# Turning K on VectorE in 32x32 blocks instead of on TensorE, in a decode step with a cached attention window

## The chip, the cores and the metric

One core of one Trainium2 chip. The metric is the device time of one execution in microseconds (us), the median of several executions. The kernel before takes 384.67 us (384.57 to 384.93 in 4 executions). The kernel before ran again in every round of experiments and took 384.67 to 384.78 us each time, so medians of different rounds can be set side by side.

## The reference, cut to what matters

```python
B, Sq, D = 4, 1, 576;  Hq, Hkv, Sk, Dh = 32, 16, 16384, 128     # bf16
W = min(4096, max(256, Sk // 4))                                # 4096 keys are looked at
q = (layernorm(x) @ wq)                                         # 32 heads of 128
k = k_cache[:, :, Sk - W:, :] ; v = v_cache[:, :, Sk - W:, :]   # each serves two q heads
p = softmax(q @ k.T * Dh ** -0.5) ;  o = p @ v
h = x + o @ wo
out = h + ((relu(n @ W_gate) * (n @ W_up)) @ W_down)            # n = layernorm(h)
```

Nearly all bytes are the window of K and V: 4 batches of 16 heads of 4096 keys of 128 values, 134 MB of the 160 MB that are read.

## The kernel before

K and V come in tiles of 4 MB (four heads of one batch), through a ring of four slots in SBUF. Partition `4*p + a` of a tile holds 128 keys of head `a`, one after the other (a load row of 32 KB).

```python
src = cache[b, 4*qd:4*qd+4, SK-WIN:SK, :].rearrange("a (p t) d -> p a (t d)", p=32)
place((kind, g), off, TILE, ("TR", 4*g+3) if kind == "K" else ("PV", 4*g+3),   # who frees the slot
      lambda e: e.dma_start(out=arena[:, off:off+TILE], in_=src), key=f"slot{s}")
```

QK needs K with the head dimension on the partitions. TensorE turns K in 128x128 pieces, and a permutation in place of the identity also sorts the keys by head. VectorE and ScalarE copy the pieces from PSUM to SBUF by turns:

```python
pe(("TRJ", i, j), lambda e: e.transpose(out=bankb[TRB[j]][:, u*128:(u+1)*128], in_=kn[:, t, :],
                                        identity=perm.rearrange("p a k -> p (a k)")), deps)      # L425
if j % 2 == 0: dve(("EV", i, j), lambda e: e.tensor_copy(out=dst, in_=src), deps)                # L439
else:          act(("EV", i, j), lambda e: e.copy(out=dst, in_=src), deps)                       # L441
# QK: 32 columns of q, four matmuls abreast in four column groups
bank[4+w][32*j:32*j+32, :], lhsT=qTm[:, b, 4*qd+a, :], rhs=k[:, j, :, a, :]                      # L457
# P: exp writes every score four times, TensorE turns it, VectorE masks it while copying
dve(("PM", b, r), lambda e: e.tensor_tensor(out=dst, in0=src, in1=msk, op=ALU.mult), ...)        # L487
```

[... cut: constants, projections of q, softmax weights, output selection, the gated layer ...]

Of the kernel before, what the change touches and what calls it, by code (L numbers as in the profile page):

```python
# [6 lines left out]
ALU = mybir.AluOpType  # L7
# [4 lines left out]
B = 4  # L12
# [9 lines left out]
NUNIT = 4 * NTILE  # L22
# [5 lines left out]
KTW = 8192  # L28
# [86 lines left out]
def bass_sequential_preLN__sliding_block_cached__glu_gated_reglu__decode_kernel(  # L115
# [12 lines left out]
    with ExitStack() as es:  # L128
# [12 lines left out]
        arena = sb("arena", [128, 2 * KTW + NSLOT * TILE], BF16)  # L141
# [6 lines left out]
        c_m4 = sb("c_m4", [128, 4, 32], FP32)  # L148
        c_qm = sb("c_qm", [128, 4, 32], FP32)
        c_e8 = sb("c_e8", [128, 8, 16], FP32)  # L150
        c_s4 = sb("c_s4", [128, 4, 4], FP32)
        perm = sb("perm", [128, 4, 32], BF16)
        m4 = sb("m4", [128, 4], FP32)
        par = sb("par", [128, 2], FP32)
        am8 = sb("am8", [128, 8], FP32)
# [16 lines left out]
        qTm = sb("qTm", [128, B, KVH, 32], BF16)  # L172
        stat = sb("stat", [128, B, 8], FP32)
        gm4 = sb("gm4", [1, 128], FP32)
        fq = sb("fq", [128, 4], FP32)
# [19 lines left out]

        kT = [arena[:, i * KTW:(i + 1) * KTW] for i in range(2)]
        slot0 = 2 * KTW

# [3 lines left out]
        TRB = (0, 1, 2, 3)  # L202
        s_ps = psb[:, 4:6, :].rearrange("p a b -> p (a b)")
        o_ps = bank[6]
        m_ps = bank[7]
        mb_ps = bankb[7]
# [25 lines left out]
        def add_kv(kind, g):  # L232
            b, qd = divmod(g, 4)
            s = ring_slot()
            off = slot0 + s * TILE
            cache = A_k_cache if kind == "K" else A_v_cache
            src = cache[b, 4 * qd:4 * qd + 4, SK - WIN:SK, :].rearrange("a (p t) d -> p a (t d)", p=32)
            place((kind, g), off, TILE, ("TR", 4 * g + 3) if kind == "K" else ("PV", 4 * g + 3),
                  lambda e: e.dma_start(out=arena[:, off:off + TILE], in_=src), key=f"slot{s}")
# [19 lines left out]
        for blk in range(2 * KTW // 64):  # L259
            owner[blk] = "QKEND"  # L260
# [24 lines left out]
        def kv(kind, i):  # L285
            off = land[(kind, i // 4)]
            return arena[:, off:off + TILE].rearrange("p (t d) -> p t d", d=DH)

# [5 lines left out]
        pool("c_perm0", lambda e: e.memset(perm[:, :, :], 0.0))  # L294
        pool("c_perm", lambda e: e.affine_select(out=perm[:, :, :], in_=perm[:, :, :], pattern=[[-1, 4], [-4, 32]],
                                                 compare_op=ALU.not_equal, fill=1.0, base=0, channel_multiplier=1), ["c_perm0"])
# [6 lines left out]
                                                compare_op=ALU.not_equal, fill=1.0, base=0, channel_multiplier=1), ["c_m40"])  # L303
        pool("c_ones", lambda e: e.memset(ones_f[:, :], 1.0))
# [20 lines left out]
        for j in range(4):  # L325
            pool(f"c_same{j + 1}", lambda e, j=j: e.affine_select(out=sameh[:, :, :], in_=sameh[:, :, :], pattern=[[0, 4], [-1, 32]],
                                                                compare_op=ALU.not_equal, fill=0.25, base=-32 * j,
                                                                channel_multiplier=1), [f"c_same{j}"])

        pool("c_toq0", lambda e: e.memset(toq[:, :, :, :], 0.0))  # L330
        for q in range(4):
# [10 lines left out]
        dve("c_am8", lambda e: e.tensor_copy(out=am8[:, :].rearrange("p (a h) -> p a h", h=2),  # L342
                                             in_=bass.AP(tensor=m4, offset=0, ap=[[4, 128], [1, 4], [0, 2]])), ["c_m4"])
        dve("c_qTm", lambda e: e.memset(qTm[:, :, :, :], 0.0))
# [23 lines left out]
        def pe_q():  # L368
# [4 lines left out]
            for c in range(DC):  # L373
                pe("TP1", lambda e, c=c: e.transpose(out=tpv[:, 32 + c * 4:32 + (c + 1) * 4],
                                                     in_=chunk(x_bf, xd_bf[:, :, :].rearrange("b r a -> b (r a)"), c),
                                                     identity=ident_b[0:B, 0:B]))
            for c in range(DC):
# [7 lines left out]
            for bk in range(2):  # L385
                for s in range(4):
                    blk = bk * 4 + s
                    pe(("QT", blk), lambda e, blk=blk: e.transpose(out=mb_ps[:, blk * 128:(blk + 1) * 128],
                                                                   in_=p_sb[:, blk * 128:(blk + 1) * 128], identity=ident_b[:, :]),
                       [f"qev{bk}"] if s == 0 else [])  # L390

        def dve_q():
# [5 lines left out]
            dve("xT", lambda e: e.tensor_copy(out=xT[:, :, :], in_=tpv[:, 32:52].rearrange("p (c b) -> p c b", b=B)))  # L398
            dve("qev0", lambda e: e.tensor_copy(out=p_sb[:, 0:512], in_=bank[4]), ["QMM"])
            for s in range(8):  # L400
                hh4, bk = s % 4, s // 4
                off = 34 * (bk * 8 + hh4 // 2) + hh4 % 2
                dst = bass.AP(tensor=qTm, offset=off, ap=[[B * KVH * 32, 128], [68, 4], [KVH * 32, B]])
                dve("qTm", lambda e, dst=dst, s=s: e.tensor_copy(  # L404
                    out=dst, in_=mb_ps[:, s * 128:(s + 1) * 128].rearrange("p (g b) -> p g b", b=32)[:, :, 0:4]),
                    [("QT", 7), "c_qTm"])
# [5 lines left out]
        def pe_tr(i):  # L412
            kn = kv("K", i)
            for j in range(4):
                for u in range(8):
                    t = j * 32 + i % 4 * 8 + u
                    deps = []
                    if u == 0:
                        deps = [("L", "K", i // 4)] if j == 0 else []
                        if i == 0:  # L420
                            deps.append("c_perm")
                        else:
                            deps.append(("EV", i - 1, j))
                    last = j == 3 and u == 7
                    o = pe(("TRJ", i, j), lambda e, j=j, u=u, t=t: e.transpose(  # L425
                        out=bankb[TRB[j]][:, u * 128:(u + 1) * 128], in_=kn[:, t, :],
                        identity=perm[:, :, :].rearrange("p a k -> p (a k)")), deps)
                    if last:
                        P.names[("TR", i)] = o

        def evac(i, j):
            lo = j * 2048 + i % 2 * 1024
            dst = kT[i // 2 % 2][:, lo:lo + 1024]
            src = bankb[TRB[j]][:, 0:1024]
            deps = [("TRJ", i, j)]
            if i >= 4:
                deps.append(("QK", i // 2 - 2))
            if j % 2 == 0:
                dve(("EV", i, j), lambda e: e.tensor_copy(out=dst, in_=src), deps)  # L439
            else:  # L440
                act(("EV", i, j), lambda e: e.copy(out=dst, in_=src), deps)  # L441

        def pe_qk(dd):
            g, w = divmod(dd, 2)
            b, qd = divmod(g, 4)
            k = kT[dd % 2].rearrange("p (j t a k) -> p j t a k", j=4, t=16, a=4)
            for a in range(4):
                for j in range(4):
                    deps = []
                    if a == 0:  # L450
                        deps.append(("EV", 2 * dd + 1, j))
                        if qd == 0 and j == 0:
                            if b == 0:
                                deps += ["qTm", "qev0", "qev1"]
                            else:
                                deps += [("EXP", b - 1, w), ("MAX", b - 1)]
                    o = pe(("QK", dd), lambda e, a=a, j=j: e.matmul(  # L457
                        bank[4 + w][32 * j:32 * j + 32, :], lhsT=qTm[:, b, 4 * qd + a, :], rhs=k[:, j, :, a, :],
                        start=(qd == 0 and a == 0), stop=(qd == 3 and a == 3), skip_group_check=True), deps)
            P.names["QKEND"] = o  # L460

        def softmax(b, w):
            if w == 0:
                dve(("MAX", b), lambda e: e.tensor_reduce(out=stat[:, b, 0:1], in_=s_ps, axis=AX.X, op=ALU.max, negate=True),  # L464
                    [("QK", 8 * b + 7)])
                dve(("NB", b), lambda e: e.tensor_scalar(out=stat[:, b, 1:2], in0=stat[:, b, 0:1], scalar1=SCALE, scalar2=None,  # L466
                                                         op0=ALU.mult), [("MAX", b)])
            act(("EXP", b, w), lambda e: e.activation(  # L468
                out=p_sb[:, 2048 * w:2048 * w + 2048].rearrange("p (k a) -> p k a", a=4),
                in_=bass.AP(tensor=psb, offset=(4 + w) * 512, ap=[[4096, 128], [1, 512], [0, 4]]), func=ACT.Exp,  # L470
                bias=stat[:, b, 1:2], scale=SCALE, accum_out=stat[:, b, 2 + 3 * w:3 + 3 * w]),
                [("NB", b), ("PT", b - 1, 3) if b else ("QT", 7)])

        def put_pT(b, r):
            for tl in range(8):
                deps = []
                if tl == 0:
                    deps = [("EXP", b, r // 2)]
# [246 lines left out]
```

## Time and profile before

| | before |
|---|---|
| time, median | 384.67 us |
| load queue busy, share of 16 engines' span | 97.4% |
| mean rate of the loads | 418 GB/s |
| PE, VectorE (DVE), ScalarE (ACT) busy | 65%, 42%, 38% |

These are lines of the profile's page of the kernel before. In the second part of the page each digit is the busy share of one of 40 slices of the span, in tenths. The groups at the end have columns: line, engine, operation, output from input, shapes, count, then busy time (us) and mean ns of one, then the idle time of the engine just before them and what ended most of it.

```profile
PE 248.7 (65%) x3781; PEld 185.9 (49%) x3781; DVE 159.0 (42%) x277; ACT 146.4 (38%) x162; POOL 8.7 (2%) x36
...
DVE  3342565665342434774432426752516454002220
...
DMA  8999999999999999999999999999999999999992
GB/s 329 439 433 432 410 421 437 434 433 433 425 423 433 427 433 435 427 420 433 437 430 435 424 428 427 427 428 439 437 432 415 421 436 451 416 431 426 416 411 113
...
q1 hardware_dynamic: 6352, 159.59, 97.4%
...
DMA 69%; PE 27%; DVE 2%; SPq 1%; ACT 1%; issue 0%
...
L425 PE MATMUL psb<-sb_perm,sb_arena 128*128 128x128 bf16 x2048 | 140.3, 235 | 74.0 <-DMA sb_arena<-in_A_k_cache_dram 73.8
L441 ACT COPY sb_arena<-psb 128x1024 bf16<-128x1024 bf16 x128 | 123.0, 1021 | 141.1 <-PE psb L425 141.1
...
L439 DVE COPY sb_arena<-psb 128x1024 bf16<-128x1024 bf16 x128 | 87.0, 689 | 112.1 <-PE psb L425 111.6
...
L512 DVE TENSOR_TENSOR sb_o_tmp<-psb,sb_qm 128x512 f32<-128x512 f32 x16 | 11.1, 692 | 41.2 <-PE psb L505 41.2
L487 DVE TENSOR_TENSOR sb_pp<-psb,sb_am 128x1024 bf16<-128x1024 bf16 x16 | 19.6, 1223 | 16.2 <-PE psb L480 16.2
...
L516 DVE TENSOR_REDUCE sb_o_sel<-sb_o_tmp 128x128 f32<-128x512 f32 x16 | 16.4, 1024 | 0.5
```

The loads never stop: the DMA row is 9 from the second slice to the last but one. PE waits for K's loads (74 us before L425); the issue of loads waits for free slots too (144.7 us on L425), but it runs so far ahead (a K tile lands 28.3 us after its issue in the median, a V tile 33.6) that the loads themselves never run out. L512 and L516 handle the same 512 elements per partition. L512 reads them in order and takes 0.69 us; L516 reads its SBUF input at a stride of 512 bytes and takes 1.02 us.

One line of the groups by shape: 32 bf16 values written 64 bytes apart took 0.29 us.

```profile
L560 DVE CAST sb_oT<-psb 128x32 bf16<-128x32 f32 x4 | 1.2, 292 | 0.8 <-PE psb L556 0.8
```

### The profile page before, as it was taken

Reading aid. Unit: us, or ns where it says so; the run is one execution under the profiler, and the core shown is the slowest. Engines: PE = TensorE matmul, PEld = TensorE weight load, DVE = VectorE, ACT = ScalarE, POOL = GpSimd, SP = SyncE. Lnnn points to the kernel's source line nnn. Section 1 sums busy time; section 2 is a strip of 40 time slices with the busy share of each in tenths; the row PEclk is TensorE's granted clock in tenths of the full one; section 3 lists DMA queues with packets and bytes.
Section 4 is the critical chain, followed back from the end, with each engine's and each line's share of the span. In section 5 each row is a group of like instructions: output and inputs, shape, how many; then the busy total and the mean of one; then the engine's idle time right before and its main releaser. Section 6 shows DMA issues by size and latency. Waiting matters only on the chain.

```text
span 382.6 us, 8170 instructions
## 1 busy us (share of the span) xinstructions
PE 248.7 (65%) x3781; PEld 185.9 (49%) x3781; DVE 159.0 (42%) x277; ACT 146.4 (38%) x162; POOL 8.7 (2%) x36
## 2 busy tenths in 40 slices
PE   0664999779492938893947667966759366026753
PEld 0643788557371726672726455745546222003532
DVE  3342565665342434774432426752516454002220
ACT  3341688836161524762433428542525401000010
POOL 7100000000000000000000000000000000000000
PEclk9997999999888796999796969996969657555597
DMA  8999999999999999999999999999999999999992
GB/s 329 439 433 432 410 421 437 434 433 433 425 423 433 427 433 435 427 420 433 437 430 435 424 428 427 427 428 439 437 432 415 421 436 451 416 431 426 416 411 113
DMA packets 6408, 160.09 MB, mean 418 GB/s; under 512 B 740, under 2 KB 744, under 8 KB 1384
## 3 DMA queue, kind: packets, MB, share of 16 engines
q1 hardware_dynamic: 6352, 159.59, 97.4%
q8 instruction: 29, 0.48, 0.5%
q14 instruction: 3, 0.02, 0.0%
q10 hardware_dynamic: 24, 0.01, 0.0%
HBM read 159.58 MB, written 0.00 MB: 417 GB/s over the span
## 4 chain that ended last, share of the span: by engine, by line
DMA 69%; PE 27%; DVE 2%; SPq 1%; ACT 1%; issue 0%
DMA sb_arena<-in_A_k_cache_dram 53%; PE psb L425 18%; DMA sb_arena<-in_B_W_down_dram 8%; DMA sb_arena<-in_A_v_cache_dram 8%; PE psb L457 5%; PE psb L505 2%; PE psb L480 1%; DVE sb_pp L487 1%; ACT sb_pp L468 1%; SPq L280 0%; DVE sb_stat L464 0%; DVE sb_o_sel L516 0%; PE psb L539 0%; PE psb L530 0%; DVE sb_o_tmp L512 0%
## 5 line engine op out<-in xcount | busy, mean ns | idle before, releaser
L425 PE MATMUL psb<-sb_perm,sb_arena 128*128 128x128 bf16 x2048 | 140.3, 235 | 74.0 <-DMA sb_arena<-in_A_k_cache_dram 73.8
L441 ACT COPY sb_arena<-psb 128x1024 bf16<-128x1024 bf16 x128 | 123.0, 1021 | 141.1 <-PE psb L425 141.1
L425 PEld LDWEIGHTS psb<-sb_perm,sb_arena 128*128 128x128 bf16 x2048 | 131.5, 106 | 89.3 <-DMA sb_arena<-in_A_k_cache_dram 79.8
L439 DVE COPY sb_arena<-psb 128x1024 bf16<-128x1024 bf16 x128 | 87.0, 689 | 112.1 <-PE psb L425 111.6
L505 PE MATMUL psb<-sb_arena,sb_pp 128*32 128x512 bf16 x512 | 35.9, 425 | 19.9 <-DMA sb_arena<-in_A_v_cache_dram 19.9
L457 PE MATMUL psb<-sb_arena,sb_qTm 128*32 128x512 bf16 x512 | 38.0, 423 | 0.9 <-DVE sb_qTm L404 0.9
L505 PEld LDWEIGHTS psb<-sb_arena,sb_pp 128*32 128x32 bf16 x512 | 12.9, 104 | 36.3 <-DMA sb_arena<-in_A_v_cache_dram 20.9
L512 DVE TENSOR_TENSOR sb_o_tmp<-psb,sb_qm 128x512 f32<-128x512 f32 x16 | 11.1, 692 | 41.2 <-PE psb L505 41.2
L487 DVE TENSOR_TENSOR sb_pp<-psb,sb_am 128x1024 bf16<-128x1024 bf16 x16 | 19.6, 1223 | 16.2 <-PE psb L480 16.2
L480 PE MATMUL psb<-sb_ident_b,sb_pp 128*128 128x128 bf16 x128 | 11.5, 242 | 15.8 <-DVE sb_pp L487 8.3
L468 ACT ACTIVATE sb_pp<-psb,sb_stat 128x2048 bf16<-128x2048 f32 x8 | 15.8, 1975 | 9.7 <-DVE sb_stat L466 9.7
L457 PEld LDWEIGHTS psb<-sb_arena,sb_qTm 128*32 128x32 bf16 x512 | 11.6, 103 | 14.8 <-issue 6.2
L480 PEld LDWEIGHTS psb<-sb_ident_b,sb_pp 128*128 128x128 bf16 x128 | 8.6, 108 | 18.8 <-ACT sb_pp L468 8.1
L516 DVE TENSOR_REDUCE sb_o_sel<-sb_o_tmp 128x128 f32<-128x512 f32 x16 | 16.4, 1024 | 0.5
L612 ACT COPY sb_pp<-psb 128x288 f32<-128x288 f32 x1 | 0.4, 399 | 36.2 <-PE psb L607 36.2
L654 PE MATMUL psb<-sb_arena,sb_hnT 128*32 128x384 bf16 x120 | 7.5, 421 | 4.1 <-DVE sb_hnT L639 2.2
L654 PEld LDWEIGHTS psb<-sb_arena,sb_hnT 128*32 128x32 bf16 x120 | 4.1, 121 | 7.2 <-DMA sb_arena<-in_B_W_up_dram 2.3
L464 DVE TENSOR_REDUCE sb_stat<-psb 128x1 f32<-128x1024 f32 x4 | 4.9, 1221 | 4.6 <-PE psb L457 4.6
L687 PE MATMUL psb<-sb_arena,sb_pp 128*32 128x144 bf16 x144 | 3.7, 251 | 4.1 <-DMA sb_arena<-in_B_W_down_dram 3.6
L534 ACT ACTIVATE sb_stat<-sb_stat 128x1 f32<-128x1 f32 x4 | 0.9, 213 | 13.1 <-DVE sb_stat L532 13.1
L661 DVE TENSOR_TENSOR sb_pp<-psb,sb_pp 128x384 bf16<-128x384 f32 x3 | 1.5, 551 | 9.6 <-PE psb L654 9.6
L687 PEld LDWEIGHTS psb<-sb_arena,sb_pp 128*32 128x32 bf16 x144 | 2.6, 105 | 5.1 <-DMA sb_arena<-in_B_W_down_dram 4.6
(128 smaller groups left out, 78.7 us busy)
## 6 DMA issues: line engine op xcount, KB each, us to landing
sb_arena<-in_A_k_cache_dram SPq DMA_DIRECT2D x16, 4096.0 KB, 28.3
sb_arena<-in_A_v_cache_dram SPq DMA_DIRECT2D x16, 4096.0 KB, 33.6
sb_arena<-in_A_wo_dram SPq DMA_DIRECT2D x1, 4608.0 KB, 20.7
sb_arena<-in_B_W_gate_dram SPq DMA_DIRECT2D x1, 4608.0 KB, 34.1
sb_arena<-in_B_W_up_dram SPq DMA_DIRECT2D x1, 4608.0 KB, 43.5
sb_arena<-in_A_wq_dram SPq DMA_DIRECT2D x1, 4096.0 KB, 23.0
sb_arena<-in_B_W_down_dram SPq DMA_DIRECT2D x3, 1296.0 KB, 30.0
sb_arena<-in_B_W_down_dram SPq DMA_DIRECT2D x1, 864.0 KB, 31.6
```

The lines of the kernel that those rows point to most:

```text
L425: o = pe(("TRJ", i, j), lambda e, j=j, u=u, t=t: e.transpose(out=bankb[TRB[j]][:, u * 128:(u + 1) * 128], in_=kn[:, t, :], identity=perm[: ...
L439: dve(("EV", i, j), lambda e: e.tensor_copy(out=dst, in_=src), deps)
L441: act(("EV", i, j), lambda e: e.copy(out=dst, in_=src), deps)
L457: o = pe(("QK", dd), lambda e, a=a, j=j: e.matmul(bank[4 + w][32 * j:32 * j + 32, :], lhsT=qTm[:, b, 4 * qd + a, :], rhs=k[:, j, :, a, :], ...
L468: act(("EXP", b, w), lambda e: e.activation(out=p_sb[:, 2048 * w:2048 * w + 2048].rearrange("p (k a) -> p k a", a=4), in_=bass.AP(tensor=p ...
L480: pe(("PT", b, r), lambda e, tl=tl: e.transpose(out=mb_ps[:, tl * 128:(tl + 1) * 128], in_=p_sb[:, (r * 8 + tl) * 128:(r * 8 + tl + 1) * 128],
L487: dve(("PM", b, r), lambda e: e.tensor_tensor(out=dst, in0=src, in1=msk, op=ALU.mult), [("PT", b, r), "c_am8", ("PV", 16 * b - 1) if b els ...
L505: pe(("PV", i), lambda e, j=j, lo=lo, pm=pm, tb=tb: e.matmul(o_ps[32 * j:32 * j + 32, :], lhsT=pT[:, pm:pm + 32], rhs=v[:, lo:lo + 512], s ...
L512: dve(("OS", g), lambda e: e.tensor_tensor(out=o_tmp[:, :].rearrange("p (t d) -> p t d", t=4), in0=o_ps.rearrange("p (t d) -> p t d", t=4) ...
L516: dve(("OSEL", g), lambda e: e.tensor_reduce(out=o_sel[:, qd, :], in_=o_tmp[:, :].rearrange("p (t d) -> p d t", t=4), axis=AX.X, op=ALU.ad ...
L654: pe(("GU", g, c // 4), lambda e, g=g, m=m, j=j, lo=lo, c=c: e.matmul(bank[3 * g + m][32 * j:32 * j + 32, 0:384], lhsT=hnT[:, c if c < 4 e ...
L687: pe("DOWN", lambda e, j=j, r=r, n=n, wv=wv: e.matmul(bank[0][32 * n:32 * n + 32, 0:144], lhsT=hhT[:, r * 128 + 32 * j:r * 128 + 32 * j + 32],
```

## The change

The intent: take 2048 PE transposes, their 256 copies and P's detour through PSUM away. A bf16 pair is taken as one 32-bit word, and VectorE turns K in place in blocks of 32 by 32 words. After it, each quadrant of 32 partitions holds 32 pairs of the head dimension for its own keys, so QK uses a block-diagonal q (one block for each quadrant). Within a block the words of the four heads come interleaved; the transpose writes them sorted by head, so that QK can read the keys of one head together. P is turned in the same way. The diff, cut to its core:

```diff
-            place((kind, g), off, TILE, ("TR", 4 * g + 3) if kind == "K" else ("PV", 4 * g + 3),
+            place((kind, g), off, TILE, ("QK", g, 1) if kind == "K" else ("PV", g),
...
-                    o = pe(("TRJ", i, j), lambda e, j=j, u=u, t=t: e.transpose(   # and the copies EV
+        def turn_k(g, w):                                                         # w: half of a tile
+            k = arena[:, land[("K", g)] + w * QWW:][:, 0:QWW].bitcast(FP32)
+            dst = k.rearrange("p (n a k) -> p n k a", a=4, k=8)
+            src = k.rearrange("p (n k a) -> p n k a", a=4, k=8)
+            dve(("TRA", g, w), lambda e: e.transpose(out=dst, in_=src), [("L", "K", g)] if w == 0 else [])
...
-                        bank[4 + w][32 * j:32 * j + 32, :], lhsT=qTm[:, b, 4 * qd + a, :], rhs=k[:, j, :, a, :],
+                    off = land[("K", g)] + w * QWW + cb // 2 * 64 + 16 * a + cb % 2
+                    pe(("QK", g, w), lambda e, ...: e.matmul(
+                        bank[SB[b % 2] + w], lhsT=arena[:, wo_:wo_ + 128],          # 128x128, block diagonal
+                        rhs=bass.AP(tensor=arena, offset=off, ap=[[AW, 128], [128, 64], [2, 8]]),
...
+            for w in range(2):                                                     # softmax: a mask in the bias
+                for a in range(4):
+                    act(("EXP", b, w), lambda e, w=w, a=a: e.activation(
+                        out=p_sb[:, 1024 * a + 512 * w:][:, 0:512], in_=bank[SB[b % 2] + w], ...
...
+        def turn_p(b, w):
+            dst = bass.AP(tensor=pp, offset=512 * w, ap=[[8192, 128], [8, 64], [1024, 4], [1, 8]])
+            src = p_sb.rearrange("p (a t k) -> p t k a", a=4, k=8)[:, 64 * w:64 * (w + 1), :, :]
+            dve(("PTR", b, w), lambda e: e.transpose(out=dst, in_=src), ...)
```

In `turn_k` consecutive words of the stream go to addresses 8 words, that is 32 bytes, apart (`a` is the innermost loop and has a step of 8 words).

## The prediction

> **What bounds the kernel now.** The load stream. The page's DMA row stands at 9 in nearly all 40 slices, the load queue was busy for 97.4% of 16 engines' span, and 160 MB moved at a mean of 418 GB/s (411 to 439 in most slices). A 4 MB K or V tile takes about 9.8 us (estimate: 4.19 MB at 428 GB/s). The chain of waits is 69% DMA; its PE pieces (27%) only release ring slots while other tiles are still arriving (28 us from issue to landing, about three tiles deep). PE (65%), VectorE (42%) and ScalarE (38%) have slack. Nothing on the compute engines can win 2%: the bytes don't change and the rate is already flat.
>
> **What the change removes and adds.** Removed: 2048 PE transposes of K (140 us PE), their copies (87 us VectorE, 123 us ScalarE), 128 PE transposes of P (11.5 us), their masked copies (19.6 us VectorE). Added on VectorE: per K tile two in-place transposes of 4096 fp32 words per partition; per batch two of 2048 bf16. QK becomes 512 full-width matmuls of 512 columns that no longer run four abreast: 0.23 us each (64 transposes of 128 columns took 3.68 us), 7 us per tile, up to twice that at the halved clock, against 2 us.
>
> **The disputed term is the transpose's rate.** VectorE takes about 1.04 ns per element plus 0.15 us (the 1024-element max: 1.22 us; the 512-element multiply: 0.69 us). At that rate half a tile takes 4.4 us (estimate), a K tile 8.8. With output selection (1.7 us) and a share of P, max and weights, VectorE then needs about 13 of the 19.6 us in which one K and one V tile arrive: hidden. But the sorting by head writes consecutive words 32 bytes apart. [...] the o_sel reduction, 512 elements read at a stride of 512 bytes, takes 1.02 us instead of about 0.68, or 1.7 ns each; a strided 32-element bf16 write took 0.29 us where about 0.18 was due. At 1.7 ns half a tile is 7 us, a K tile 14; P's strided transposes 3.6 us each. A batch then costs VectorE about 14x4 + 7 + 7 + softmax waits of 7 or more = 77 us or more, against 78 us of loads. K tiles come without V tiles at first, slots free late, and the queue runs dry after batch boundaries: 10 to 35 us lost. At 2 ns or more VectorE bounds outright (430 us and up).
>
> **Start.** K's slot is freed after QK instead of after transposing; the first QK needs q, so tile K3 is issued near 41 us instead of near 22, just before the queue would dry up (0 to 3 us lost). The tail (weights) stays load bound.
>
> **Prediction.** Full rate: 384 to 388 us. Line penalty: 395 to 425. Worse: 430 to 480. I lean slightly to a penalty: 394 us, 80% range 381 to 450. Chances: faster by over 2% 0.02, within 2% 0.43, slower 0.55.
>
> **What would show it.** Mean time of the K transpose: 4.4 us (hidden) or 7 and up (exposed). DMA row: 9 throughout, or gaps after each fourth K tile. VectorE share: about 50% or above 75%. The queue's own waits: QK, long. PE busy below 200 us, ScalarE below 40. The first tile's QK ending near 41 us.
>
> **What would make it wrong.** Words written 32 bytes apart at full rate or far worse; QK's stride-2 moving reads slow; loads slowed by VectorE's traffic.

The sum: 14 x 4 + 7 + 7 + 7 = 77 us of VectorE for a batch, against 78 us of loads. Its 1.7 ns rests on the two strided operations named there (1.02 and 0.29 us); that K's transposes would pay the same was the estimate. "Line penalty" is only the name of the outcome at that rate. "The halved clock" is a granted clock of 0.50: in the trace of before, 32 of K's transposes took 3.60 us at 0.50 (from 35.32 us) and 64 took 3.75 us at 1.00 (from 40.41 us).

## The result, and the profile after

421.79 us (419.46 to 422.74, 4 executions) against 384.67 us. The ratio is 1.095, 95% interval 1.092 to 1.098. Ratios in this document are the mean time of one kernel's fast runs over that of the other's in the same rounds, so they are not quite the ratio of the medians that are quoted. Executions over 1.5% slower than the fastest of the same kernel are left out of the means.

| | before | after |
|---|---|---|
| time, median | 384.67 us | 421.79 us |
| load queue busy | 97.4% | 89.7% |
| PE busy | 248.7 us | 221.9 us |
| VectorE busy | 159.0 us | 312.8 us |
| ScalarE busy | 146.4 us | 33.8 us |

The page of the changed kernel, the lines that answer to those of before:

```profile
PE 221.9 (53%) x1629; PEld 92.2 (22%) x1629; DVE 312.8 (74%) x158; ACT 33.8 (8%) x94; POOL 16.2 (4%) x38
...
DVE  0888999499989894999898949998999656402101
...
DMA  8999899990993999999949999999399998999995
GB/s 350 409 440 445 356 434 415 400 398 3 400 400 111 440 447 409 436 450 365 434 161 446 403 448 450 406 404 431 165 415 429 450 428 332 393 417 448 432 413 212
...
q1 hardware_dynamic: 6352, 159.59, 89.7%
...
DVE 49%; DMA 30%; PE 13%; issue 7%; SPq 1%
...
L422 DVE STREAM_TRANSPOSE sb_arena<-sb_arena 128x4096 f32<-128x4096 f32 x32 | 235.9, 7416 | 6.1 <-DMA sb_arena<-in_A_k_cache_dram 6.1
L439 PE MATMUL psb<-sb_arena 128*128 128x512 bf16 x512 | 151.1, 460 | 74.8 <-DVE sb_arena L422 72.7
...
L469 DVE STREAM_TRANSPOSE sb_pp<-sb_pp 128x2048 bf16<-128x2048 bf16 x8 | 28.5, 3608 | 0.0
```

The chain that ended last was 69% DMA and is now 49% VectorE. VectorE's row is 8 or 9 for three quarters of the span. The loads have holes, at the slices of 3, 111, 161 and 165 GB/s: two after the first batch's maximum (83 us) and then one in each of the next two batches. One K transpose takes 7.42 us, and 32 of them take 236 us. Before L439, PE no longer waits for a load but for VectorE.

The windows view gives busy time by stretch; here the columns are the stretch and its length, busy us (and instructions) of each engine, granted clock, DMA share and GB/s. First comes the stretch from the first to the last K transpose, then the time between the maxima of consecutive batches.

```profile
core 0: us, PE busy (x) PEld busy (x) DVE busy (x) ACT busy (x) POOL busy (x), PEclk, DMA share, GB/s
14.60:331.80 317.20, 179.98 (x1008) 69.61 (x1008) 284.82 (x99) 21.50 (x65) 3.54 (x10) 0.81 0.89 379
83.10:166.30 83.20, 47.57 (x232) 18.01 (x232) 73.73 (x26) 6.51 (x20) 0.00 (x0) 0.75 0.76 321
166.30:251.80 85.50, 47.63 (x296) 18.72 (x296) 75.38 (x29) 6.52 (x20) 0.00 (x0) 0.82 0.93 393
251.80:337.10 85.30, 47.34 (x296) 18.62 (x296) 75.34 (x29) 5.46 (x16) 0.00 (x0) 0.82 0.93 394
```

VectorE was busy for 284.8 of 317.2 us (90%) of that stretch, though only for 74% of the span. A batch takes 85 us, of which VectorE works for 75. What it does in the other 10 us stands in the view of waits (columns: who waited for whom, us in total, times, longest):

```profile
DVE sb_o_tmp L490 <- PE psb L482: 25.0, 5, 16.9
DVE sb_stat L446 <- PE psb L439: 21.4, 4, 5.4
...
DVE sb_arena L422 <- DMA sb_arena<-in_A_k_cache_dram: 6.1, 4, 1.7
```

Once a batch the max (L446) stands first in VectorE's queue and waits 5 us for the last QK (21.4 us in 4 waits); the trace shows VectorE idle in them (5.41 us before 83.11 us), with the next transposes right behind the softmax's steps. (16.9 us of the first line are one wait at the end, for the last V tile.)

The same maxima say where the 37.3 us of the two spans (419.9 - 382.6) were lost: the first stands 14.6 us later than before (83.1 against 68.5), the three batches after it took 26.1 us more (254.0 against 227.9), and the stretch after the last maximum 3.4 us less.

### The profile page after: what moved, and what is told of

It reads as the page before. It is cut to its first block, busy times and chain, and to the rows that moved or that the text cites. A ratio compares the mean times of both kernels' runs of the same rounds, so it can differ in the third digit from the quotient of the medians.

```text
span 419.9 us, 3670 instructions
## 1 busy us (share of the span) xinstructions
PE 221.9 (53%) x1629; PEld 92.2 (22%) x1629; DVE 312.8 (74%) x158; ACT 33.8 (8%) x94; POOL 16.2 (4%) x38
## 3 DMA queue, kind: packets, MB, share of 16 engines
q1 hardware_dynamic: 6352, 159.59, 89.7%
## 4 chain that ended last, share of the span: by engine, by line
DVE 49%; DMA 30%; PE 13%; issue 7%; SPq 1%
DVE sb_arena L422 36%; DMA sb_arena<-in_A_k_cache_dram 16%; PE psb L439 9%; DMA sb_arena<-in_B_W_down_dram 8%; DVE sb_pp L469 6%; DMA sb_arena<-in_A_v_cache_dram 5%; DVE sb_o_sel L494 2%; PE psb L482 2%; DVE sb_o_tmp L490 1%; DVE sb_stat L446 1%; DVE sb_selw L510 0%; PE psb L519 0%; PE psb L507 0%; PE psb L502 0%; PE psb L448 0%
## 5 line engine op out<-in xcount | busy, mean ns | idle before, releaser
L422 DVE STREAM_TRANSPOSE sb_arena<-sb_arena 128x4096 f32<-128x4096 f32 x32 | 235.9, 7416 | 6.1 <-DMA sb_arena<-in_A_k_cache_dram 6.1
L439 PE MATMUL psb<-sb_arena 128*128 128x512 bf16 x512 | 151.1, 460 | 74.8 <-DVE sb_arena L422 72.7
L439 PEld LDWEIGHTS psb<-sb_arena 128*128 128x128 bf16 x512 | 55.7, 114 | 167.7 <-DVE sb_arena L422 84.2
L460 ACT ACTIVATE sb_pp<-psb,sb_stat 128x512 bf16<-128x512 f32 x32 | 21.5, 697 | 287.4 <-DVE sb_stat L455 287.4
L469 DVE STREAM_TRANSPOSE sb_pp<-sb_pp 128x2048 bf16<-128x2048 bf16 x8 | 28.5, 3608 | 0.0
L446 DVE TENSOR_REDUCE sb_stat<-psb 128x1 f32<-128x1024 f32 x4 | 4.9, 1224 | 21.4 <-PE psb L439 21.4
L502 PE MATMUL psb<-sb_stat,sb_sameh 128*128 128x1 f32 x8 | 2.1, 336 | 21.1 <-DVE sb_stat L500 21.1
L519 PE MATMUL psb<-sb_o_sel,sb_selw 128*32 128x32 f32 x128 | 2.2, 221 | 18.4 <-DVE sb_o_sel L494 18.4
L382 PE MATMUL psb<-sb_arena,sb_xnT 128*32 128x512 bf16 x32 | 3.6, 631 | 8.9 <-DMA sb_arena<-in_A_wq_dram 8.9
L298 POOL MEMSET sb_arena<- 128x8192 f32 x1 | 6.9, 6924 | 0.0
L460 ACT ACTIVATION_READ_ACCUMULATOR sb_pp<-psb,sb_stat 128x1 f32 x32 | 6.9, 216 | 0.0
```

Source lines behind the costliest of these rows:

```text
L298: pool("c_qW", lambda e: e.memset(arena[:, 0:2 * QWW].bitcast(FP32), 0.0))
L422: dve(("TRA", g, w), lambda e: e.transpose(out=dst, in_=src), [("L", "K", g)] if w == 0 else [])
L439: pe(("QK", g, w), lambda e, off=off, wo_=wo_, qd=qd, first=first, last=a == cb == 3: e.matmul(bank[SB[b % 2] + w], lhsT=arena[:, wo_:wo_ ...
L446: dve(("MAX", b), lambda e: e.tensor_reduce(out=stat[:, b, 0:1], in_=s_ps, axis=AX.X, op=ALU.max, negate=True), [("QK", 4 * b + 3, 1)])
L460: act(("EXP", b, w), lambda e, w=w, a=a: e.activation(out=p_sb[:, 1024 * a + 512 * w:][:, 0:512], in_=bank[SB[b % 2] + w], func=ACT.Exp, b ...
L469: dve(("PTR", b, w), lambda e: e.transpose(out=dst, in_=src), [("EXP", b, w), ("PV", 4 * b - 1) if b else "QMM"])
```

## The experiments

The theory (W): the sorted write sets the transpose's time, because consecutive words go to addresses 32 bytes apart; VectorE then can't keep pace with the loads, and loads stop. Rivals: (F) 32-bit transposes are slow in themselves; (I) turning in place makes reads and writes collide; (T) the traffic of loads and matmuls slows VectorE; (Q) not VectorE, but the late release of K's slots behind QK at the halved clock (after the change 0.50 at 34 to 38 us and at 86 to 94 us).

All runs passed the comparison with the reference, also those whose keys are in a wrong order. So that comparison does not see the order of keys, and it proves nothing for the variants that are called right here; for `pairs` and `keyblocks` (and the changed kernel) the index maps were replayed on random data, and q, K, V came out as attention to rounding. `unsorted` is right by the same index arithmetic.

### micro: the disputed cost by itself

After the result is copied out, VectorE does fourteen operations on 4096 elements of each partition, each twice, with the loads and matmuls finished:

```diff
+        nat = lambda t, a: t.rearrange("p (n k a) -> p n k a", a=a, k=32 // a)
+        srt = lambda t, a: t.rearrange("p (n a k) -> p n k a", a=a, k=32 // a)
+        mic("m1", lambda e: e.transpose(out=nat(wA, 4), in_=nat(wA, 4)))       # L684 contiguous
+        mic("m2", lambda e: e.transpose(out=srt(wA, 4), in_=nat(wA, 4)))       # L685 32 bytes apart, as in the kernel
+        mic("m3", lambda e: e.transpose(out=srt(wA, 16), in_=nat(wA, 16)))     # L686 8 bytes apart
+        mic("m4", ...srt(wA, 8)...)  mic("m5", ...srt(wA, 2)...)               # L687 16, L688 64 bytes apart
+        mic("m6", lambda e: e.transpose(out=srt(wB, 4), in_=nat(wA, 4)))       # L689 32 bytes apart, not in place
+        mic("m7", lambda e: e.transpose(out=nat(wB, 4), in_=srt(wA, 4)))       # L690 read 32 bytes apart
+        ... m9 to m11 fp32 copies (L692 contiguous, L693 strided write), m12 to m14 bf16 transposes (L696 strided write, L697 strided read)
```

> The changed kernel, with VectorE operations on 4096 fp32 words per partition added after the result is copied out (each twice, in a chain), so the disputed cost stands alone with loads and matmuls finished. Theory W (the 32-byte write stride sets the cost): transpose with contiguous writes 4.3 to 4.6 us, with writes 32 bytes apart 7.2 to 7.5 us as in the kernel, with 8 bytes apart 4.3 to 4.6, with 16 and 64 bytes apart about 7; out of place with stride also 7.2 to 7.5; a plain fp32 copy with the same write stride also about 7 against 2 to 4.4 contiguous. Rival F (fp32 transposes are slow in themselves): all transposes near 7.4, also the contiguous one. Rival I (in-place read and write collide): in place near 7.4 with any stride, out of place 4.4. Rival T (traffic of loads and matmuls slows it): all near 4.4 here, the strided ones too. Time of the whole: that of the changed kernel plus the sum of these (about 140 to 180 us).

Measured (a single execution, so its state is unknown; only groups within it are compared; groups by shape in the tail; busy us, then mean ns of one):

```profile
L696 DVE STREAM_TRANSPOSE sb_arena<-sb_arena 128x4096 bf16<-128x4096 bf16 x2 | 35.9, 17971 | 0.1
L687 DVE STREAM_TRANSPOSE sb_arena<-sb_arena 128x4096 f32<-128x4096 f32 x2 | 14.9, 7432 | 0.1
L685 DVE STREAM_TRANSPOSE sb_arena<-sb_arena 128x4096 f32<-128x4096 f32 x2 | 14.9, 7431 | 0.1
L689 DVE STREAM_TRANSPOSE sb_arena<-sb_arena 128x4096 f32<-128x4096 f32 x2 | 14.9, 7428 | 0.1
L690 DVE STREAM_TRANSPOSE sb_arena<-sb_arena 128x4096 f32<-128x4096 f32 x2 | 14.9, 7428 | 0.1
L697 DVE STREAM_TRANSPOSE sb_arena<-sb_arena 128x4096 bf16<-128x4096 bf16 x2 | 14.2, 7093 | 0.1
L688 DVE STREAM_TRANSPOSE sb_arena<-sb_arena 128x4096 f32<-128x4096 f32 x2 | 14.0, 7012 | 0.1
L686 DVE STREAM_TRANSPOSE sb_arena<-sb_arena 128x4096 f32<-128x4096 f32 x2 | 8.9, 4446 | 0.1
...
L684 DVE STREAM_TRANSPOSE sb_arena<-sb_arena 128x4096 f32<-128x4096 f32 x2 | 8.9, 4446 | 0.1
...
L693 DVE COPY sb_arena<-sb_arena 128x4096 f32<-128x4096 f32 x2 | 7.7, 3854 | 0.1
L692 DVE COPY sb_arena<-sb_arena 128x4096 f32<-128x4096 f32 x2 | 4.6, 2294 | 0.1
```

Contiguous, or words 8 bytes apart: 4.446 us. Words written 16 or 32 bytes apart, or read 32 bytes apart: 7.43 us; at 32 bytes in place or not. 64 bytes apart, back and forth between two rows of words (L688), 7.01 us. F falls (the contiguous transpose is fast), I falls (L689 is not in place), T falls (no traffic, and still 7.43). A plain copy shows it too, though not at the size that was expected (3.85 against 2.29 us, not 7): the ratio is the same 1.7, but a word 32 bytes from the one before it costs 0.94 ns in the copy and 1.81 ns in the transpose, so it is not one fixed time for each such word. One surprise: bf16 values written 16 bytes apart took 17.97 us, 4.4 ns each, more than twice the cost of 32-bit words; bf16 values read 2048 bytes apart and written contiguously (L697) took only 7.09 us. So between 8 and 16 bytes lies the step: up to 8 bytes apart the transpose of 32-bit words ran as fast as contiguously, from 16 on it did not. Why, these runs do not show.

### contig_wrong: the same kernel with contiguous writes

```diff
-            dst = k.rearrange("p (n a k) -> p n k a", a=4, k=8)
+            dst = k.rearrange("p (n k a) -> p n k a", a=4, k=8)
```

> Only the order of the K transpose's writes is changed to contiguous; QK still reads as if sorted, so the result is wrong on purpose; every instruction, wait and byte else is the same. Theory W: the K transpose takes 4.3 to 4.6 us, VectorE then needs about 61 of 78 us in a batch, the load queue is fed again, 384 to 390 us in all, load queue at 95% or more. Rival F and I: the transpose stays at 7.4 us and the time at 420 us. Rival Q (it is late release of slots behind QK at the halved clock, not VectorE): transpose faster, but the time still above 405 us.

Measured: 382.01 us (381.60 to 382.51), ratio to before 0.993 (0.992 to 0.995). Lines of its page:

```profile
DMA  8999999999999999999999999999999999999994
...
q1 hardware_dynamic: 6352, 159.59, 98.0%
...
DMA 55%; DVE 20%; PE 20%; issue 4%; SPq 1%; ACT 0%
...
L422 DVE STREAM_TRANSPOSE sb_arena<-sb_arena 128x4096 f32<-128x4096 f32 x32 | 141.5, 4434 | 58.0 <-DMA sb_arena<-in_A_k_cache_dram 58.0
```

The order of the writes is the only edit, and all of the loss is gone: the transpose takes 4.43 us, VectorE now waits for the loads, the loads have no holes. Q falls as the whole explanation: K's slots are still freed only after QK, the clock is as low (0.79 in the mean, against 0.80 in the changed kernel), and it costs nothing. What it costs while VectorE is short of time is a matter for `order` and `halves` below. The result is wrong, so this is no version to use; it is the bound of what a right one could reach.

### unsorted and pairs: can the sorting be had elsewhere?

`unsorted` writes contiguously and lets QK pick a head's keys at a stride of 16 bytes; its result is right. `pairs` keeps two words of a head together, so VectorE writes 8 bytes apart, and the exps read the scores in the order that undoes it.

```diff
 unsorted:
-            ... 16 * a + cb % 2 ...   ap=[[AW, 128], [128, 64], [2, 8]]
+            ... 2 * a + cb % 2 ...    ap=[[AW, 128], [128, 64], [8, 8]]          # and dst as in contig_wrong
 pairs:
-            dst = k.rearrange("p (n a k) -> p n k a", a=4, k=8)
+            dst = k.rearrange("p (n a k) -> p n k a", a=16, k=2)
-            ... 16 * a + cb % 2 ...   ap=[[AW, 128], [128, 64], [2, 8]]
+            ... 4 * a + cb % 2 ...    ap=[[AW, 128], [128, 64], [16, 4], [2, 2]]
```

> Contiguous writes as in contig_wrong, and QK reads each head's columns at a stride of 16 bytes instead of 4, so the result is right. If matmul reads at 16 bytes cost nothing: same as contig_wrong, 384 to 390 us. If they cost double (QK near 14 us a tile warm): 390 to 405 us, PE busy up by 60 us or more, load queue dry in the first batch only. Rivals F and I: about 420 us or more.

> A sort that keeps two consecutive words of a head together: the transpose's writes step by 8 bytes (4.45 us in the run that measured strides alone), QK reads two neighbouring words, then steps 32 bytes, and the exp reads its scores in the order that undoes the pairing. Result right by its index arithmetic. Theory W, with matmul reads at two words[...] at full rate (0.22 to 0.24 us a matmul warm): 381 to 385 us, as the wrong contiguous run (382.0). If matmul reads pay as in the 16-byte run (about 1 us a matmul): 550 us or more. If they pay half of that: 400 to 450 us.

Measured: `unsorted` 625.97 us (ratio 1.627), `pairs` 401.76 us (ratio 1.045, 1.043 to 1.046). The transpose takes 4.43 us in both. The timelines of PE (start, us, what) show runs of QK matmuls, first in the changed kernel, then in `pairs`, then in `unsorted`:

```profile
55.98 3.63 PE L439 MATMUL psb<-sb_arena 128*128 128x512 bf16 x16 [2.13 <-DVE sb_arena L422]
63.24 6.38 PE L439 MATMUL psb<-sb_arena 128*128 128x512 bf16 x16 [3.63 <-DVE sb_arena L422]
```

```profile
49.58 32.98 PE L439 MATMUL psb<-sb_arena 128*128 128x512 bf16 x76
```

```profile
49.18 33.65 PE L439 MATMUL psb<-sb_arena 128*128 128x512 bf16 x39
```

Groups of eight words side by side: 3.63 us / 16 = 0.227 us a matmul; the windows view gives a granted clock of 1.00 for this stretch ("warm" in the expectations). (6.38 / 16 = 0.40 us is the same matmul at a granted clock of 0.56.) Groups of two words, 32 bytes from start to start: 32.98 / 76 = 0.434 us, in slices whose clock digit on the page is 9 (0.9 or more) but for the last, 8. Single words, 16 bytes apart: 33.65 / 39 = 0.863 us, in slices with the digit 5 (0.5 to 0.6). The clock is a rival here, since it moved as well, but the record speaks against it: the matmul with groups of eight took no more than 0.40 us at 0.56, the first 128 QK matmuls of `pairs` took about 55.4 us (from 30.6 us to the first max at 86.05), 0.433 us each, through slices with digits from 6 to 9, and the four executions of `unsorted` took 625 to 627 us at mean clocks of 0.58 and 0.69 alike. Divided by the groups that 512 columns are read from (256 of two words, 512 single words), the two give 1.70 and 1.69 ns a group; VectorE's transpose, 7.43 us / 4096, gives 1.81 ns a word. So in these runs a matmul, too, took about 1.7 ns for each single word or group of two, where the fast matmul took 0.44 ns a column (0.227 us / 512). Two words side by side, 0.89 ns at that rate, were too few on PE, while on VectorE words 8 bytes apart still ran as fast as contiguous ones (4.43 us in `pairs`). What in PE's reads sets the 1.7 ns was not shown. `unsorted` was expected to cost at most a doubling and cost nearly four times the 0.227 us; that expectation missed. In `pairs` the cost moved to PE: QK takes 71% of an interval of one K and one V tile's load (32 x 0.434 = 13.9 us of about 19.6), which fits in the loop, but not at the start, where K tiles come without V tiles between: its first max came at 86.1 us, against 67.3 in `contig_wrong`, and this lag of 18.8 us is close to the whole difference between the two (401.8 - 382.0 = 19.8).

### dose7_wrong: the prediction's own rate

A write order with consecutive words 64 bytes apart takes 7.0 us, exactly the figure of the prediction's penalty branch. Nothing else is changed (result wrong):

```diff
-            dst = k.rearrange("p (n a k) -> p n k a", a=4, k=8)
-            src = k.rearrange("p (n k a) -> p n k a", a=4, k=8)
+            dst = k.rearrange("p (n a k) -> p n k a", a=2, k=16)
+            src = k.rearrange("p (n k a) -> p n k a", a=2, k=16)
```

> The changed kernel with a write order (consecutive words 64 bytes apart[...]) that took 7.01 us alone, that is, the 7.0 us of my prediction's penalty branch; all reads, waits and bytes unchanged, result wrong on purpose. It tells what the prediction's arithmetic gives when its rate is right. Estimate from the chain's sums: 404 to 413 us. If it is 417 us or more, the arithmetic of the rest (waits around the softmax, the ring) was short, not the rate; if under 400, the rate alone was short.

Measured: 409.56 us (409.26 to 409.92), ratio 1.065 (1.063 to 1.066).

```profile
L422 DVE STREAM_TRANSPOSE sb_arena<-sb_arena 128x4096 f32<-128x4096 f32 x32 | 223.9, 7043 | 4.8 <-DMA sb_arena<-in_A_k_cache_dram 4.8
```

Per transpose 7416 - 7043 = 373 ns, times 32 = 11.9 us of VectorE's work less, and the time fell by 12.2 us (421.79 to 409.56). At this rate VectorE's work counts one for one. The time is 24.9 us above that of the kernel before, in the middle of the 10 to 35 us that the prediction gave for its penalty branch.

### p_contig_wrong: the smaller stride, of P

```diff
-            src = p_sb.rearrange("p (a t k) -> p t k a", a=4, k=8)[:, 64 * w:64 * (w + 1), :, :]
+            src = p_sb.rearrange("p (a x) -> p a x", a=4)[:, :, 512 * w:512 * w + 512]
```

> The changed kernel with only P's transposes reading contiguously (result wrong on purpose): 2.2 to 2.3 us each instead of 3.6, 10 to 11 us of VectorE work less in all. If VectorE's work counts one for one: 409 to 412 us. If VectorE and the ring of slots wait for each other, less comes back: 413 to 419 us.

Measured: 2.28 us a transpose instead of 3.61, so 10.7 us of VectorE's work less. The time was 411.69 us in the median, but the four executions spread (406.6 to 414.0) and two of them were slow; the fast two give a ratio of 1.062 (1.057 to 1.067), 408.6 us. This agrees with one for one (about 10 to 13 us less), with less certainty than the run before.

### order, halves, order_halves: the waits beside VectorE's work

`order` turns the first half of the next K tile before the max, so the max no longer blocks VectorE while QK ends. `halves` loads and frees each tile in two halves. `order_halves` does both.

```diff
 order:
+                if g + 1 < NTILE:
+                    turn_k(g + 1, 0)
                 softmax(b)                       # and not again at the start of do_k(g + 1)
 halves:
+            for w in range(2):
+                place((kind, g, w), off + w * QWW, QWW, ("QK", g, w) if kind == "K" else ("PV", g), ...)
-            ... [("L", "K", g)] if w == 0 else [])
+            ... [("L", "K", g, w)])
```

> The changed kernel with the first half of the next K tile turned before a batch's max instead of after the softmax chain; result right, nothing else changed. Theory W with VectorE as the bound in the loop: the wait of the max for QK (5.3 us a batch) goes, three to four batches, so 400 to 408 us; VectorE idle before the max under 1 us. Rival Q: the max and with it P and V come later, so no gain or a loss: 418 to 430 us.

> The changed kernel with every K and V tile loaded as two halves; the first half of a K tile can be turned when it has landed, and its space goes back to the loads after its own QK; VectorE's work unchanged, result right. If the part of the loss beyond VectorE's work (about 20 us: 313 us of work, about 14 us ahead of the first transpose, 83 us from the last max to the end, against 420) is the ring of four slots and VectorE waiting for each other: 398 to 410 us, VectorE's waits for K loads and the load queue's waits both shorter. If it is only in-order stalls around the softmax: 416 to 421 us.

> The changed kernel with both mends at once, the next tile's first half turned before the max and tiles loaded and released by halves; VectorE's work unchanged at 313 us. Alone they gave 420.6 and 417.8. If each alone only moved a wait (from QK to K loads in the one, nothing in the other because of the order): together 398 to 411 us. If the loop is bound by VectorE's work alone: 415 to 420 us.

Measured: `order` 420.57 us (418.76 to 421.32), `halves` 417.82 us (416.97 to 418.72), both together 408.73 us (406.35 to 409.15, ratio 1.061). VectorE's work is 312 to 313 us in all three. The waits of VectorE, in `order` and then in `order_halves`:

```profile
DVE sb_o_tmp L490 <- PE psb L482: 31.4, 7, 16.3
...
DVE sb_arena L422 <- DMA sb_arena<-in_A_k_cache_dram: 11.3, 5, 3.6
...
DVE sb_stat L446 <- PE psb L439: 5.8, 1, 5.8
```

```profile
DVE sb_o_tmp L493 <- PE psb L485: 32.5, 8, 16.9
...
DVE sb_stat L449 <- PE psb L442: 6.1, 1, 6.1
```

`order` was expected to give 400 to 408 us and gave nothing: that expectation fell, and the time that was written down there for the rival came out (418 to 430 us), though not its reason, that max, P and V come later: the first max began at 84.9 us instead of 83.1, but P's transposes of the first three batches at 95.1, 182.3 and 269.6 us instead of 100.4, 186.3 and 271.8. The wait for QK went (21.4 to 5.8 us), but VectorE now waited for K's loads (6.1 to 11.3 us) and for PV (25.0 to 31.4). The sum of the three waits went only from 52.5 to 48.5 us. `halves` alone took away the wait for loads (to 0) and kept the other two (23.1 and 25.5, sum 48.6). Only both together bring the sum down, to 38.6 us, 13.9 less, and the span down by 13.2 (419.9 to 406.7). So the slots and VectorE's order hold each other: a wait removed on one side came back on the other. `halves` alone fell on the line of its expectation that meant little gain (416 to 421 us), `order_halves` on the one that meant that each alone only moved a wait (398 to 411 us). Together they win 13 of the 37 us back with the stride as it was.

### keyblocks and rows8k_wrong: a version that needs no sort

The stride comes from four heads being interleaved on the partitions. `keyblocks` lays 128 blocks of 32 neighbouring keys of one head on the partitions and the four heads side by side in the columns. The transpose is contiguous, QK reads groups of 32 words side by side (512 matmuls busy for 141.9 us, against 143.6 in `contig_wrong`), and no mask is needed in the exps:

```diff
-            src = cache[...].rearrange("a (p t) d -> p a (t d)", p=32)
+            src = cache[...].rearrange("a (p t) d -> p a (t d)", p=128)
+                  ... out=arena[:, off:off + TILE].rearrange("p (a x) -> p a x", a=4) ...
-            dst = k.rearrange("p (n a k) -> p n k a", a=4, k=8)
+            dst = k
-                        rhs=bass.AP(tensor=arena, offset=off, ap=[[AW, 128], [128, 64], [2, 8]]),
+                        rhs=bass.AP(tensor=arena, offset=off, ap=[[AW, 128], [128, 16], [2, 32]]),
+            # PV: head a in column group a; the rows of other heads get weight 0
```

> A version that needs no sort: a tile's partitions are 128 blocks of 32 neighbouring keys of one head, the four heads lie side by side in the columns (load rows of 8 KB instead of 32 KB). K's transposes write contiguously (4.45 us), QK reads four neighbouring words[...] (0.22 to 0.24 us a matmul warm), the exps need no mask and P shrinks to a quarter (P's transposes under 0.8 us each). Result right by its index arithmetic. If the write stride was the cause of the loss[...]: load bound again, 380 to 384 us, VectorE under 55%. If rows of 8 KB load more slowly: up to 395 us with the load queue at 97% or more and a lower rate. If something else of the new structure (block-diagonal q, slot release after QK) costs: above 390 us with the load queue below 95%.

Measured: 389.03 us (388.85 to 389.30), ratio 1.011 (1.010 to 1.013). That is not the expected 380 to 384 us, but it lies inside the second line of the expectation: slower rows. The page:

```profile
GB/s 312 448 408 421 421 421 422 421 422 423 422 420 421 421 421 422 422 421 421 422 421 421 421 424 421 420 422 422 421 419 424 424 419 452 402 436 426 427 421 162
...
q1 hardware_dynamic: 18640, 159.59, 98.8%
...
L420 DVE STREAM_TRANSPOSE sb_arena<-sb_arena 128x4096 f32<-128x4096 f32 x32 | 141.5, 4435 | 80.2 <-DMA sb_arena<-in_A_k_cache_dram 80.2
```

It is bound by the loads again (98.8% busy, VectorE at 51% and waiting 80 us for them), but at 421 instead of about 430 GB/s. The control `rows8k_wrong` is `contig_wrong` with each tile loaded in four pieces, so with rows of 8 KB:

```diff
+            for x in range(4):
+                place((kind, g, x), off + x * 4096, 4096, ("QK", g, x // 2) if kind == "K" else ("PV", g), ...)
```

> A control for what is left of keyblocks' time: contig_wrong (contiguous transposes, result wrong on purpose, 382.0 us) with every K and V tile loaded in four pieces of 8 KB rows, the row length of keyblocks; the transposes still wait for the whole tile. If the row length is what holds keyblocks at 389.0: 387 to 390 us, load queue at 98% or more at 410 to 415 GB/s. If not: 381 to 384 us at 420 GB/s.

Measured: 388.78 us (388.50 to 388.91), ratio 1.010 (1.009 to 1.012).

```profile
q1 hardware_dynamic: 20176, 159.59, 98.8%
```

So the row length (or the count of packets that goes with it, 20176 against 6352) accounts for what `keyblocks` lacks. The control has four loads for a tile where `keyblocks` has one, but the rate of about 421 GB/s is the same in both. No right version beat the kernel before; `keyblocks` comes within 1.1% of it and is 7.8% faster than the changed kernel (389.03 / 421.79, of different rounds). A layout with rows of 32 KB and neighbouring keys of one head on neighbouring partitions was not built, so whether a right version can reach 382 us stays open.

## Why the prediction was right or wrong

- **Right: what bounds the kernel, and that nothing could be won.** The loads did; a kernel with the stride taken away gains 0.7%, and `keyblocks`, whose result is right, loses 1.1%.
- **Right: the cause.** The prediction named the writes 32 bytes apart (on the two strided operations in its trace), said "At 1.7 ns half a tile is 7 us, a K tile 14", and for that case gaps in the DMA row, the queue waiting for QK, P's transposes at 3.6 us. Measured: 7.42 us, 14.8 us, holes in the load row, 286 us of the load queue's waits on QK (16 times), 3.61 us. (The waits on QK alone are a weak sign: `keyblocks`, which loses 1.1%, has 261 us of them, 16 times.) `contig_wrong` shows that all of the loss goes when this stride goes. `order_halves` shows that its size also hangs on the waits around it: 13 of the 37 us go without touching the stride.
- **Wrong: the size.** The prediction gave 394 us (+2.4%); it was 421.8 (+9.5%). The step that failed is the cost of the transpose, which the prediction left open between two rates, 4.4 us and 7 us for half a tile, at the end of its sum: "Full rate: 384 to 388 us. Line penalty: 395 to 425 ... I lean slightly to a penalty: 394 us". 394 lies between two outcomes and is neither; the runs showed 7.42 us for half a tile, the second rate and a little more, and a loss of 37 us. A time within 2% of before had a chance of 0.43, although the prediction itself named two measurements of strided SBUF access in the trace of before (1.02 us where 0.68 was due, 0.29 where 0.18 was due).
- **Within the branch, two terms of "14x4 + 7 + 7 + softmax waits of 7 or more = 77 us or more" were too small.** K's transposes of a batch took 8 x 7.42 = 59.4 us, not 56, since a word cost 1.8 ns and not 1.7. The rest, without P (7.2) and output selection (6.8), took 85.3 - 59.4 - 7.2 - 6.8 = 11.9 us, not 7: the max, weights and waits for PE, once a batch. So a batch took 85 us against 78 us of loads, where the sum had 77. `dose7_wrong`, at the prediction's own 7.0 us, took 409.6 us, inside the branch's 395 to 425; the measured rate adds the other 12 us.
- **Right: the first issues.** The first QK was to end "near 41 us" with the next K tile issued then; that tile and the one behind it were issued by 43.7 us, and the loads at most dipped there (356 GB/s in the fifth slice). The cost of the start came later, in the holes of the 10th and 13th slices, because four K tiles at 14.8 us each can't keep up with loads of about 9.8 us each (estimate: 4.19 MB at 428 GB/s): the first max came at 83.1 us, against 68.5 before. That is 14.6 of the 37.3 us. The prediction names it ("K tiles come without V tiles at first"), but its sum for a batch holds no term for it.
- **Wrong, without effect: PE busy "below 200 us".** It was 222. QK took 151 us for 512 matmuls, 0.295 us each instead of 0.227, and the stretch above with 0.40 us at a clock of 0.56 shows how; at 0.227 us it would have been about 187 us in all (estimate: 222 - 151 + 116). `contig_wrong` has nearly the same PE time (217 us) and no loss.
- **Right: "QK's stride-2 moving reads" were not slow**: 0.227 us a matmul. `unsorted` (0.863 us) and `pairs` (0.434 us) show what other spacings cost.

## What to carry to other kernels

Before a data movement is put on an engine because a share of busy time says that it has room, look at how far apart the words lie that it reads and writes one after the other: here, on VectorE, a transpose of 32-bit words 16 or 32 bytes apart cost 1.67 times a contiguous pass (7.43 us against 4.446) and 8 bytes apart no more than it; on PE a matmul that read single words 16 bytes apart cost 3.8 times the one that read eight side by side (0.863 us, at a clock digit of 5, against 0.227 at 1.00), and one that read two side by side 1.9 times (0.434 us). And the sort that spares the one can burden the other. A layout made by the load (here, which keys stand on which partition) can make the sort unnecessary, but look at the load's row length too (about 421 GB/s with rows of 8 KB in `keyblocks` and `rows8k_wrong`, about 430 with 32 KB). And where a forecast hangs on one disputed duration with two outcomes far apart, let the evidence choose an outcome; a number between the two is a forecast of neither.
